# Attention and two expert layers on one core: the sixteenth tile's places are scattered alone, and the list scheduler gets new gaps and due times

## The chip, the cores and the metric

The kernel runs on one core of a Trainium2 chip. Its engines are TensorE (PE, matmuls; PEld is its weight load), VectorE (DVE), ScalarE (ACT), GpSimd (POOL) and SyncE (SP), which only issues transfers here. Each takes its instructions in the order in which they stand in the program. The metric is the device time of one execution in microseconds; the time before is the median of three runs.

## The reference, cut to what matters

Three layers follow one another; all arrays are float32.

```python
# attention: B, H, S, D = 4, 8, 576, 64; block-causal mask, blocks of 64
scores = scale * np.matmul(q, k.transpose(0, 1, 3, 2))
scores = np.where(mask, scores, -1000000000.0)
attn = np.exp(scores - scores.max(-1, keepdims=True))
attn = attn / (attn.sum(-1, keepdims=True) + 1e-09)
x = (attn @ v).transpose(0, 2, 1, 3).reshape(2304, 512)
# dense layer: w_in 512 x 1024, w_out 1024 x 512
h = x @ w_in
solu = h * softmax(h)
x = ((solu - mean(solu)) / np.sqrt(var(solu) + 1e-06) * g_ln) @ w_out
# experts: 8 of 512 x 1024 x 512, one for each token
logits = normed(x) @ normed(expert_emb).T / tau
expert_idx = np.argmax(logits, axis=1); gate_w = softmax(logits)[expert_idx]
out[mask] = gate_w[mask, None] * (np.maximum(x[mask] @ w1[e], 0.0) @ w2[e])   # for each expert e
```

## The kernel before, in words

Products are made with operands split in a high and a low half, three matmuls each (`mm3`, L552 to L557; "a triple" below is one such group on 512 columns, L555, L556, L557).

**The scheduled part.** Attention runs in 36 items (`items`): scores (`attn_score`, L436) with maximum (L439), exponential (L442) and scaling by the reciprocal sum (L448, L450, then `scaled`, L232 on ACT or L234 on POOL); transposes of the probabilities (`attn_trans`, L475, split at L481 and L484); the product with the values (`attn_av`, L520). The 2304 tokens are 18 tiles of 128. Each tile goes up (`b_load`, `b_up`, keys U: eight groups of triples, then maximum L600, exponential L601, product L603, normalization on POOL L606 and L610 to L614), down (`b_down`, D: transposes L631, eight triples, the tile stored to `x2d` at L641) and through the router (`b_route`, R: transposes L666, eight small products L675 and L676, a transposition L683, logits on DVE L686 and L687). The weights of the dense layer are unpacked meanwhile (`conv_ops`, C).

**Choosing.** Tiles are chosen for in batches (`BATCH`, L647). `b_choose` part 0 takes the roots of the norms on POOL (L705), the maximum, the one-hot matrix and the gate weights on DVE (L709 to L722); part 1 sums the one-hot matrices of the tiles before on POOL (`sums`, L730 to L733), turns them into places with two small products on TensorE (`places`, L737 and L738, "the place product" below), makes addresses on DVE (L747 to L749) and writes gate weight and token number of each tile to those places in the array `meta` in DRAM, one indirect transfer of POOL for a tile (L753, a "scatter"). All scatters write `meta`, so each waits until the one before has landed. The last batch that the scheduled part places holds tiles 12 to 15. Behind tile 15 (`TCUT`), `first_ops` counts tokens by expert (L797), picks the fullest (L804 to L810, L1092 to L1096), reads the first 2 x 128 places back from `meta` (SP, L979) and gathers these tokens' rows (POOL, L987).

**What sets the order.** All of this is written as operations with a duration, an engine, the names that they read and write, and for some a second engine that may take them (`either`). `order` walks through time and gives each engine the ready operation of highest priority; it reckons with `Rates`: `hop`, the gap from one engine's end to the next one's start, `over`, an engine's own gap, `land` and `rate` of transfers. A priority is the negative of a due time, `DUE` by kind of step and item, plus the step's own place in its chain (`priorities`). The sequence that comes out is the order of the instructions on each engine; the planner's times are not used on the chip, where every instruction waits for its real inputs. The planner also gives PSUM banks, and it decides who takes an `either`.

**The expert part** (`c_all`) works on slices of 128 gathered tokens: transposes L998, up (`c_up`, triples and L1016), transposes L1027, down (`c_down`), and a scatter of the rows to the output (L1044). The tiles 16 and 17 are chosen for inside its first slices. Its order is written out by hand. "The seam" below is the stretch from the last matmul of the scheduled part to the first L998.

Of the kernel before, what the change touches and what calls it, by code (L numbers as in the profile page):

```python
# [314 lines left out]
def conv_ops(c, k, n):  # L315
# [28 lines left out]
    op("POOL", 1.28, lambda: nc.gpsimd.tensor_tensor(WL, f, WH.bitcast(F32), op=ALU.subtract), r=[an, "wh%d" % k], w=["wl%d" % k],  # L344
# [21 lines left out]
def attn_prep(c, it):  # L366
# [30 lines left out]
    either(op, "POOL", lambda eng: scaled(c, eng, H, it.R, c.qscale[:, 0:1]), ACT=.21 + .00083 * W, POOL=.27 + .00083 * W,  # L397
# [9 lines left out]
def attn_prep_v(c, it):  # L407

    op, nc = c.op, c.nc
    k, n = 2 if it.low else 5, it.vi % 2  # L410
    raw = c.vraw[n][:, 0:k]
    op("SP", .45, lambda: nc.sync.dma_start(raw, c.v[it.pair, :, 0:k]), r=["pa"], w=["Vr%d" % n], size=64 * k)
    V = raw.rearrange("p c (h d) -> p c h d", d=64)
    V2 = c.V2[n][:, 0:k]
    vh, vl = V2[:, :, :, 0:64], V2[:, :, :, 64:128]
    either(op, "POOL", lambda eng: scaled(c, eng, vh, V, 1.0), ACT=.21 + .00083 * 128 * k, POOL=.2 + .00083 * 128 * k,
           r=["pa", "Vr%d" % n], w=["Vh%d" % n])
    op("POOL", .16 + .00219 * 128 * k, lambda: nc.gpsimd.tensor_tensor(vl, V, vh.bitcast(F32), op=ALU.subtract),
       r=["pa", "Vr%d" % n, "Vh%d" % n], w=["Vl%d" % n], lock=True)
# [5 lines left out]
def attn_score(c, it, step):  # L425
# [19 lines left out]
    if step in it.norm:  # L445
# [5 lines left out]
        for j in js:  # L451
            W, P, e = it.q[j][2:5]
            f = lambda eng, j=j, P=P, o=E[:P, e:e + W]: scaled(c, eng, o, o, rs[:P, j:j + 1])
            either(op, "POOL", f, ACT=.21 + .00083 * W, POOL=.28 + .00083 * W, r=["pa", ("rs%d" % n, a, b)], w=[(en, e, e + W)])
# [41 lines left out]
def attn_av(c, it, step):  # L496
# [34 lines left out]
    if odd:  # L531
        if two:
            op("POOL", .1 + .00208 * m, lambda: nc.gpsimd.tensor_tensor(xo[0], xo[0], xo[1], op=ALU.add), r=["pa", reg[1](0, 2)],
               w=[reg[0](0, 2)], lock=True)
# [38 lines left out]
def b_load(c, t):  # L573
# [8 lines left out]
    either(op, "POOL", lambda eng: scaled(c, eng, xh, xf, 1.0), ACT=.64, POOL=.63, r=[("xf%d" % n, 0, 4)], w=["xh%d" % n])  # L582
# [4 lines left out]
def b_up(c, t):  # L587
# [30 lines left out]
    op("POOL", 1.2, variance, r=[mn + "3", mn + "5", "mhalf"], w=[mn + "8"])  # L618
# [28 lines left out]
BATCH = [0, 4, 8, 12, 16, 17, 18]  # L647
# [43 lines left out]
def b_choose(c, a, part):  # L691
# [12 lines left out]
    if part == 0:  # L704
        op("POOL", .6, lambda: G.tensor_tensor(nr[:, 0:n], nr[:, 0:n], c.halves[:, 0:n], op=ALU.pow), r=["half"],  # L705
# [5 lines left out]
        op("DVE", .42, inverse, r=["tau", ("nr%d" % x, 0, 4)], w=[nm("inv")])  # L711
# [498 lines left out]
def order(ops, rate=Rates, tail=None):  # L1210
# [49 lines left out]
    now = 0.  # L1260
    while True:
# [39 lines left out]
        o.end = t + o.dur  # L1301
        free[o.eng] = o.end + rate.over[o.eng]
# [23 lines left out]
def stages(c, dag):  # L1326
# [30 lines left out]
    for t in range(NTILE):  # L1357
# [27 lines left out]
    Z=[163.2],  # L1385
    X=[766.1],
    C=[-186.4, 225.8, -38.9, -183.2, -79.3, -57.4, -32.7, -168.4, 102.7, 37.7, 153.1, 43.3, 136.9, 366.2, 97.9, -90.8],
    A=[-40.9, -100.2, -174.4, -308., -398.2, -149.3, -202.6, 49.4, -64.5, 40.3, -41.2, 363.3, 21.7, -200.9, 37.2, 224.4, -59.4,
       274.5, 333.9, -112.2, 441.1, 305.8, 242.1, -84.4, -110.4, -102.1, 198.1, 465.9, 430.9, 458.7, 662.3, 517.2, 529., 196.4,
       514.2, 899.3],  # L1390
    S=[-105.3, -140.4, -213.8, -231.1, -388., -122.3, 102.1, 10.4, 12.7, 71.1, 251.4, 207.4, 151.4, 53.2, 121.8, 98.8, 62.,
       175.8, 211., 189.6, 142.6, -5.8, 157.5, 90.4, 141.7, 104.5, 192.9, 185., 184.7, 115.2, 275.5, 391.6, 335.6, 245.6, 431.,
       323.1],
    T=[30.1, -109.5, -53., -143.6, -202.3, -105.5, -8.9, 108.5, -79.2, 179.9, 82.8, 93.7, -18.5, 4.6, 109.8, 147., -34., -76.8,
       -72.4, -29.4, 101.6, 126.4, 163.1, 90.1, 92.4, 161.1, 197.4, 233.6, 200.8, 256.6, 187.6, 280.3, 56.8, 49.9, 214.4,
       449.2],
    V=[-34.1, -143.2, 70.5, -217.7, -287., 46.9, 110.9, 24.8, 106.3, 53.2, -70.7, 168.4, 113.6, 22.7, 57.3, 147.5, 83.2, -106.6,
       -17.7, 28.5, 135.5, 142.7, 103.2, 218.3, 263.9, 191.7, 213.3, 155.6, 343., 349.7, 446.3, 630.1, 446.1, 332.9, 538.2,
       328.6],
    U=[-9.8, 72.8, -76.1, 195.2, -188.3, 52.3, 251.4, 242.9, 243.8, 325.4, 349.3, 352., 420.6, 454.4, 337.6, 239.3, 446.5,  # L1400
       856.5],
    D=[128.7, 209.1, 150.2, 236.2, 248., 260.7, -167.9, 257.5, 295.3, 373.9, 443., 589.1, 568.9, 326.3, 481.1, 143., 45.7,
       789.9],
    R=[-21.6, 42.5, 70.4, 237.8, 90.2, -283.1, -132.9, 25.4, 127.2, 774.6, 352.1, 140.5, 216.2, 934.2, 450.8, -49.4, 37.1,
       433.8],)
# [156 lines left out]
```

## Time and profile before

| what | value |
|---|---|
| median of 3 runs | 828.52 us (827.42 to 830.83) |
| profiled execution | 826.53 us, its span 824.6 us |
| TensorE busy in the span | 717.0 us (87%) |
| DVE, ACT, POOL busy | 471.0, 432.2, 330.4 us (57%, 52%, 40%) |
| mean granted TensorE clock | 0.946 |

The profile is of one execution. Busy times are sums over its span; the time of a single stretch is read from the windows and timelines below, since the stretches have different limits. "Idle before" in a row is the time in which the engine stood before this instruction, and behind the arrow is what ended it. The granted clock is the share of TensorE's full 2.4 GHz; 0.50 is its lower level, 1.2 GHz.

### The profile page before, as it was taken

To read this page: it belongs to the slowest core of one execution; us is meant where nothing else is said; L and a number is where in the kernel's file an instruction comes from. 1 tells how busy PE (TensorE), PEld (TensorE's weight loads), DVE (VectorE), ACT (ScalarE), POOL (GpSimd) and SP (SyncE) were. 2 spreads that over 40 slices of the span, in tenths; PEclk is the share of its full clock that TensorE was granted. 3 is DMA by queue.
4 is the path that set the end of the run, shared out by engine and by line. 5 is a ranking of instruction groups with operands and counts; after the bars stand their busy time and mean duration, and the time that the engine had idled before them with its cause. 6 is when DMAs were issued, how large, how long until landed. Compare 5 with 4: busy or idle time off the path is not lost. (4 is left out here: it accounts for less than half of the span.)

```text
span 824.6 us, 12837 instructions
## 1 busy us (share of the span) xinstructions
PE 717.0 (87%) x3830; PEld 576.5 (70%) x3830; DVE 471.0 (57%) x1040; ACT 432.2 (52%) x997; POOL 330.4 (40%) x512
## 2 busy tenths in 40 slices
PE   3869768889999899989999998099899989989994
PEld 2657556678777688768888786077688867867883
DVE  6778768777668587856884576053121256266221
ACT  6776668586786577756783564022121256165211
POOL 5564546666474465655454542212111101111110
PEclk9979779999999899999999999589999998999998
DMA  7974675534352435551112530108611137348110
GB/s 246 274 200 142 188 201 138 152 97 119 99 151 61 82 92 155 144 115 37 42 49 66 155 114 23 28 4 286 226 53 39 41 135 271 114 160 301 40 41 23
DMA packets 59891, 101.02 MB, mean 122 GB/s; under 512 B 14289, under 2 KB 26225, under 8 KB 59793
## 3 DMA queue, kind: packets, MB, share of 16 engines
q1 hardware_dynamic: 55856, 89.44, 37.2%
q0 software_dynamic: 3936, 10.51, 3.8%
q8 instruction: 32, 0.52, 0.3%
q14 instruction: 67, 0.54, 0.2%
HBM read 65.42 MB, written 15.11 MB: 98 GB/s over the span
## 5 line engine op out<-in xcount | busy, mean ns | idle before, releaser
L555 PE MATMUL banks<-wexp,workr 128*128 128x512 f32 x320 | 134.7, 421 | 3.7 <-ACTq L1056 3.0
L556 PE MATMUL banks<-wexp,workr 128*128 128x512 f32 x320 | 128.8, 402 | 3.7 <-DVEq L1056 3.7
L557 PE MATMUL banks<-wexp,workr 128*128 128x512 f32 x320 | 128.7, 402 | 0.0
L555 PE MATMUL banks<-win,workr 128*128 128x512 f32 x288 | 124.4, 432 | 0.7 <-ACT att L442 0.7
L543 DVE TENSOR_TENSOR workr<-banks,workr 128x512 fp32r<-128x512 f32 x61 | 42.2, 691 | 135.7 <-ACT workr L542 111.2
L436 PE MATMUL banks<-attr 128*64 128x512 f32 (+5 forms) x384 | 89.9, 361 | 30.2 <-DVE attr L392 11.5
L556 PE MATMUL banks<-win,workr 128*128 128x512 f32 x288 | 115.6, 402 | 0.0
L557 PE MATMUL banks<-win,workr 128*128 128x512 f32 x288 | 115.4, 401 | 0.0
L442 ACT ACTIVATE att<-banks,att 64x576 f32<-64x576 f32 (+4 forms) x160 | 90.1, 567 | 34.7 <-DVE att L439 33.1
L439 DVE TENSOR_REDUCE att<-banks 64x1 f32<-64x576 f32 (+4 forms) x160 | 82.7, 537 | 40.0 <-PE banks L436 37.4
L436 PEld LDWEIGHTS banks<-attr 128*128 128x128 f32 (+1 forms) x384 | 60.0, 196 | 46.0 <-POOL attr L388 11.5
L1016 ACT ACTIVATE work<-banks 128x512 f32<-128x512 f32 x40 | 23.9, 597 | 118.3 <-PE banks L557 118.2
L520 PE MATMUL banks<-attr 128*128 128x320 f32 (+9 forms) x504 | 71.9, 292 | 14.1 <-DVE attr L484 10.6
L1044 POOL DMA_INDIRECT out<-work x20 | 20.3, 1017 | 157.9 <-DVE work L1043 145.9
L475 PE MATMUL banks<-work,att 128*128 128x128 f32 (+1 forms) x480 | 72.5, 282 | 12.2 <-ACT att L232 4.5
L481 ACT ACTIVATE attr<-banks 128x320 fp32r<-128x320 f32 (+4 forms) x160 | 62.8, 434 | 35.1 <-PE banks L475 32.7
L520 PEld LDWEIGHTS banks<-attr 128*128 128x128 f32 (+1 forms) x504 | 65.9, 163 | 21.2 <-DVE attr L484 6.3
L484 DVE TENSOR_TENSOR attr<-banks,attr 128x320 fp32r<-128x320 f32 (+4 forms) x160 | 72.7, 481 | 11.5 <-ACT attr L481 9.8
L542 ACT ACTIVATE workr<-banks 128x512 fp32r<-128x512 f32 x61 | 36.5, 598 | 73.8 <-PE banks L1027 48.6
L475 PEld LDWEIGHTS banks<-work,att 128*128 128x128 f32 (+1 forms) x480 | 52.4, 150 | 31.6 <-issue 8.1
L556 PEld LDWEIGHTS banks<-wexp,workr 128*128 128x128 f32 x320 | 62.0, 194 | 17.0 <-DVEq L1056 5.2
L555 PEld LDWEIGHTS banks<-wexp,workr 128*128 128x128 f32 x320 | 61.7, 193 | 16.8 <-ACTq L1056 4.1
(210 smaller groups left out, 1289.6 us busy)
## 6 DMA issues: line engine op xcount, KB each, us to landing
raw<-in_w SPq DMA_DIRECT2D x28, 1024.0 KB, 8.1
attr<-attr SPq DMA_DIRECT2D x128, 144.0 KB, 3.4
att<-in_kq SPq DMA_DIRECT2D x32, 288.0 KB, 3.7
att<-in_v SPq DMA_DIRECT2D x16, 320.0 KB, 3.6
x2d<-work SPq DMA_DIRECT2D x19, 256.0 KB, 3.0
work<-xT SPq DMA_DIRECT2D x14, 256.0 KB, 3.2
work<-in_w_in SPq DMA_DIRECT2D x5, 512.0 KB, 5.7
xT<-att SPq DMA_DIRECT2D x16, 160.0 KB, 2.6
```

What stands on the lines that cost most here:

```text
L436: nc.tensor.matmul(ps.ap[:P, a:b], st[:, q0:q0 + P], mv[:, k0 + a:k0 + b], start=y == 0, stop=y == 1, skip_group_check=True)
L439: op("DVE", .15 + .00104 * W, lambda j=j, W=W, P=P, ps=ps: nc.vector.reduce_max(nm[:P, j:j + 1], ps.ap[:P, 0:W], axis=X, negate=True), r=[ ...
L442: op("ACT", .45 + .00086 * W, lambda j=j, W=W, P=P, e=e, ps=ps: nc.scalar.activation(E[:P, e:e + W], ps.ap[:P, 0:W], AF.Exp, bias=nm[:P, j ...
L475: nc.tensor.transpose(ps.ap[:, o:o + Q], E[:Q, a:a + 128], c.ident[:Q, :Q])
L481: op("ACT", .18 + .00083 * nch * Q, lambda src=src, dh=dh: nc.scalar.activation(dh(), src(), AF.Copy), r=["pa", ps], w=[("TH", a, b) for a ...
L484: lambda src=src, dh=dh, dl=dl: nc.vector.tensor_tensor(dl(), src(), dh().bitcast(F32), op=ALU.subtract),
L520: nc.tensor.matmul(o, a, b, start=k == 0, stop=k == len(mm) - 1, skip_group_check=True)
L542: h = c.nc.scalar.activation(H, ps, AF.Copy)
L543: return h, c.nc.vector.tensor_tensor(L, ps, H.bitcast(F32), op=ALU.subtract)
L555: nc.tensor.matmul(o, ah, bh, start=first, stop=False)
L556: nc.tensor.matmul(o, ah, bl, start=False, stop=False)
L557: nc.tensor.matmul(o, al, bh, start=False, stop=last)
```

## The change

One entry is added to `BATCH`, so that tile 15 has a batch of its own: its roots, sums, place product, addresses and scatter are separate operations now, and those of tiles 12 to 14 no longer wait for tile 15. The rest changes numbers of the planner: durations of some operations (the square root of a batch by its size, ACT's scaling 0.085 us more, POOL's steps), smaller hops between engines, an extra gap ahead of POOL, a negative own gap of ACT and DVE, landing 2.5 and rate 280 instead of 1.9 and 230, 0.07 us when TensorE changes from one kind of step to another, no hop behind operations without an engine, and a new value for every due time.

```diff
-BATCH = [0, 4, 8, 12, 16, 17, 18]
+BATCH = [0, 4, 8, 12, 15, 16, 17, 18]
...
-    either(op, "POOL", lambda eng: scaled(c, eng, H, it.R, c.qscale[:, 0:1]), ACT=.21 + .00083 * W, POOL=.27 + .00083 * W,
+    either(op, "POOL", lambda eng: scaled(c, eng, H, it.R, c.qscale[:, 0:1]), ACT=.295 + .00083 * W, POOL=.27 + .00083 * W,
...
-        op("POOL", .6, lambda: G.tensor_tensor(nr[:, 0:n], nr[:, 0:n], c.halves[:, 0:n], op=ALU.pow), r=["half"],
+        op("POOL", .4 + .16 * n, lambda: G.tensor_tensor(nr[:, 0:n], nr[:, 0:n], c.halves[:, 0:n], op=ALU.pow), r=["half"],
...
-    hop = dict(PE=.25, ACT=.1, DVE=.1, POOL=.12, SP=.1)
-    land, rate = 1.9, 230.
-    over = dict(PE=0., ACT=.02, DVE=.02, POOL=.03, SP=0.)
+    hop = dict(PE=.25, ACT=.04, DVE=.05, POOL=.04, SP=.06)
+    over = dict(PE=0., ACT=-.1, DVE=-.08, POOL=.08, SP=0.)
+    pool, turn, land, rate = .12, .07, 2.5, 280.
...
-            s.avail = max(s.avail, o.end + (0. if same else rate.hop[o.eng] if o.eng in rate.hop else 0.))
+            s.avail = max(s.avail, o.end + (0. if same or o.eng is None else rate.hop[o.eng] + (rate.pool if s.eng == "POOL" else 0.)))
...
+        if e == "PE":
+            o.end += rate.turn if o.key[0] != kind else 0.
+            kind = o.key[0]
...
-    Z=[163.2],
-    X=[766.1],
+    Z=[586.3],
+    X=[2200.3],
...
```

**The order on POOL at the end of the scheduled part.** The first row below is the last of tile 17's small steps. L705 are the roots of tiles 16 and 17, L730 x1, L732 x3 and L733 the sums of the batch 12 to 15, the other L730 and L733 those of tiles 16 and 17; L753 x1 and x3 are the four scatters of tiles 12 to 15. Behind them come the branch on a wrongly guessed first expert, which begins with a load of ti, and the gathers (L987).

```order
L613 TENSOR_SCALAR work<-work 128x1
L705 TENSOR_TENSOR work<-work 128x1
L730 COPY work<-work 128x8
L732 TENSOR_TENSOR work<-work 128x8 x3
L733 TENSOR_TENSOR work<-work 128x8
L730 COPY work<-work 128x8
L753 DMA meta<-work 18432x2
L705 TENSOR_TENSOR work<-work 128x1
L733 TENSOR_TENSOR work<-work 128x8
L730 COPY work<-work 128x8
L753 DMA meta<-work 18432x2 x3
L770 TENSOR_LOAD ti
```

Now the same stretch begins with tile 17's normalization (L606); the first scatter of tiles 12 to 14 stands two rows ahead of these.

```order
L606 TENSOR_SCALAR work<-work 128x1024
L753 DMA meta<-work 18432x2
L610 TENSOR_SCALAR work<-work 128x1
L611 TENSOR_SCALAR work<-work 128x1
L612 TENSOR_TENSOR work<-work 128x1
L613 TENSOR_SCALAR work<-work 128x1
L705 TENSOR_TENSOR work<-work 128x1
L753 DMA meta<-work 18432x2
L730 COPY work<-work 128x8
L733 TENSOR_TENSOR work<-work 128x8
L730 COPY work<-work 128x8
L753 DMA meta<-work 18432x2
```

The second and third scatter of the batch 12 to 14 stand among L606, L610 to L613 and the root of tile 15 (L705); one scatter, that of tile 15, is left behind its sums (L730, L733; the second L730 is tile 16's). The root of tile 16 and the first gather follow it, the second gather stands behind the branch.

**The order on TensorE at the seam.** Before, the place product of the batch 12 to 15 (32 columns) and the count (L797) stand here, then three triples of tile 17, and the expert part begins (L998, behind the branch).

```order
L797 MATMUL banks<-work 128x8
L555 MATMUL banks<-win,workr 128x512
L556 MATMUL banks<-win,workr 128x512
L557 MATMUL banks<-win,workr 128x512
L555 MATMUL banks<-win,workr 128x512
L556 MATMUL banks<-win,workr 128x512
L557 MATMUL banks<-win,workr 128x512
L555 MATMUL banks<-win,workr 128x512
L556 MATMUL banks<-win,workr 128x512
L557 MATMUL banks<-win,workr 128x512
L818 UNCONDITIONAL_BRANCH
L998 MATMUL banks<-work 128x128 x4
```

Now the place product of tile 15 (8 columns) and the count stand earlier; these rows follow the count, and the transposes L666 are of tile 16's router.

```order
L797 MATMUL banks<-work 128x8
L555 MATMUL banks<-win,workr 128x512
L556 MATMUL banks<-win,workr 128x512
L557 MATMUL banks<-win,workr 128x512
L666 MATMUL banks<-work 128x128 x4
L555 MATMUL banks<-win,workr 128x512
L556 MATMUL banks<-win,workr 128x512
L557 MATMUL banks<-win,workr 128x512
L555 MATMUL banks<-win,workr 128x512
L556 MATMUL banks<-win,workr 128x512
L557 MATMUL banks<-win,workr 128x512
L555 MATMUL banks<-win,workr 128x512
```

Between the count and L998 there are eight triples now, one group of four transposes, eight router products and one L683, where there were three triples. Between the place product of tiles 12 to 14 and that of tile 15 stand fifteen triples, five groups of four transposes, eight router products and one L683. From the first L998 on TensorE's rows are the same in both.

In the whole order, L234 (scaling on POOL) stands 138 times before and 117 now, L232 (the same on ACT) 95 and 115 times; TensorE goes from one kind of step to another 406 times before and 390 now; behind the last L520 stand 88 triples of the dense layer before and 104 now.

## Rows read from the trace of the kernel before

**Rows 1.** Stage windows: start:end, length, busy us (count) by engine, PE clock, DMA share, GB/s

```profile
0.00:11.53 11.53, 0.00 (x0) 0.03 (x1) 6.95 (x17) 6.79 (x11) 6.34 (x24) 1.00 0.85 258
11.53:175.00 163.47, 127.04 (x683) 99.20 (x683) 124.16 (x269) 112.51 (x290) 94.20 (x134) 0.90 0.67 185
175.00:435.00 260.00, 249.20 (x1504) 205.21 (x1505) 187.19 (x425) 180.38 (x470) 146.97 (x247) 0.97 0.36 93
...
513.30:535.40 22.10, 0.00 (x0) 0.00 (x0) 1.60 (x13) 1.51 (x4) 7.09 (x9) 0.59 0.11 29
535.40:541.40 6.00, 5.28 (x18) 3.86 (x19) 1.18 (x4) 0.79 (x2) 0.30 (x1) 0.50 0.09 28
541.40:824.60 283.20, 257.50 (x1206) 206.15 (x1204) 103.92 (x197) 91.05 (x151) 42.85 (x43) 0.97 0.37 126
```

**Rows 2.** TensorE timeline at the seam: start, us, instruction, idle before and releaser

```profile
510.84 0.19 PE L737 MATMUL banks<-work 128*128 128x32 bf16 x1
...
512.89 0.40 PE L557 MATMUL banks<-win,workr 128*128 128x512 f32 x1
535.43 1.12 PE L998 MATMUL banks<-work 128*128 128x128 f32 x4 [22.14 <-DMA work<-x2d,work]
```

**Rows 3.** GpSimd timeline at the seam and behind it

```profile
513.53 1.08 POOL L753 DMA_INDIRECT meta<-work  x1 [3.05 <-DVE work L715]
...
518.09 1.07 POOL L753 DMA_INDIRECT meta<-work  x1 [2.19 <-DMA meta<-work]
522.12 0.98 POOL L753 DMA_INDIRECT meta<-work  x1 [2.97 <-DMA meta<-work]
526.31 0.97 POOL L753 DMA_INDIRECT meta<-work  x1 [3.21 <-DMA meta<-work]
531.86 1.06 POOL L987 DMA_INDIRECT work<-x2d,work  x1 [4.57 <-SPq L818]
...
541.10 1.02 POOL L753 DMA_INDIRECT meta<-work  x1 [6.88 <-DVE work L749]
```

**Rows 4.** DMA issues from 513 to 536 us: queue, count, median us to landing

```profile
meta<-work POOLq DMA_INDIRECT x4, 3.8
```

**Rows 5.** TensorE timeline: the place product of tile 16

```profile
539.96 0.23 PE L737 MATMUL banks<-work 128*128 128x8 bf16 x1
```

**Rows 6.** TensorE timeline: transposes, triples and router products

```profile
489.76 0.60 PE L631 MATMUL banks<-work 128*128 128x128 f32 x4
490.12 0.48 PE L555 MATMUL banks<-win,workr 128*128 128x512 f32 x1
...
490.89 0.39 PE L555 MATMUL banks<-win,workr 128*128 128x512 f32 x1
...
491.60 0.40 PE L555 MATMUL banks<-win,workr 128*128 128x512 f32 x1
...
495.81 0.22 PE L675 MATMUL banks<-workr 128*16 128x128 f32 x1
...
496.29 0.61 PE L666 MATMUL banks<-work 128*128 128x128 f32 x4
```

**Rows 7.** GpSimd timeline: the normalization of tile 17 and a root

```profile
500.06 1.13 POOL L606 TENSOR_SCALAR work<-work 128x1024 f32<-128x1024 f32 x1 [1.16 <-DVE work L616]
502.48 0.34 POOL L610 TENSOR_SCALAR work<-work 128x1 f32<-128x1 f32 x1 [1.29 <-ACT work L617]
...
503.84 0.26 POOL L613 TENSOR_SCALAR work<-work 128x1 f32<-128x1 f32 x1
...
514.90 0.57 POOL L705 TENSOR_TENSOR work<-work 128x1 f32<-128x1 f32 x1 [0.29 <-ACT work L725]
```

**Rows 8.** Waits of TensorE, 0 to 180 us: us in total, times, longest

```profile
PE banks L520 <- DVE attr L484: 10.6, 8, 2.1
PE banks L436 <- DMA attr<-attr: 5.2, 4, 2.5
```

**Rows 9.** Groups by line: ACT's scaling of scores

```profile
L232 ACT ACTIVATE att<-att 128x256 f32<-128x256 f32 (+4 forms) x72 | 40.9, 594 | 11.6 <-DVE att L450 11.0
```

More of the change, by code (lines that the diff above doesn't have):

```diff
@@ L343, in conv_ops @@
     op("ACT", .63, lambda: nc.scalar.activation(WH, f, AF.Copy), r=[an], w=["wh%d" % k])
-    op("POOL", 1.28, lambda: nc.gpsimd.tensor_tensor(WL, f, WH.bitcast(F32), op=ALU.subtract), r=[an, "wh%d" % k], w=["wl%d" % k],
+    op("POOL", 1.1, lambda: nc.gpsimd.tensor_tensor(WL, f, WH.bitcast(F32), op=ALU.subtract), r=[an, "wh%d" % k], w=["wl%d" % k],
        lock=True)
@@ L415, in attn_prep_v @@
     vh, vl = V2[:, :, :, 0:64], V2[:, :, :, 64:128]
-    either(op, "POOL", lambda eng: scaled(c, eng, vh, V, 1.0), ACT=.21 + .00083 * 128 * k, POOL=.2 + .00083 * 128 * k,
+    either(op, "POOL", lambda eng: scaled(c, eng, vh, V, 1.0), ACT=.295 + .00083 * 128 * k, POOL=.2 + .00083 * 128 * k,
            r=["pa", "Vr%d" % n], w=["Vh%d" % n])
@@ L453, in attn_score @@
             f = lambda eng, j=j, P=P, o=E[:P, e:e + W]: scaled(c, eng, o, o, rs[:P, j:j + 1])
-            either(op, "POOL", f, ACT=.21 + .00083 * W, POOL=.28 + .00083 * W, r=["pa", ("rs%d" % n, a, b)], w=[(en, e, e + W)])
+            either(op, "POOL", f, ACT=.295 + .00083 * W, POOL=.28 + .00083 * W, r=["pa", ("rs%d" % n, a, b)], w=[(en, e, e + W)])
 def attn_trans(c, it, step):
@@ L532, in attn_av @@
         if two:
-            op("POOL", .1 + .00208 * m, lambda: nc.gpsimd.tensor_tensor(xo[0], xo[0], xo[1], op=ALU.add), r=["pa", reg[1](0, 2)],
+            op("POOL", .21 + .00208 * m, lambda: nc.gpsimd.tensor_tensor(xo[0], xo[0], xo[1], op=ALU.add), r=["pa", reg[1](0, 2)],
                w=[reg[0](0, 2)], lock=True)
@@ L581, in b_load @@
         at += w
-    either(op, "POOL", lambda eng: scaled(c, eng, xh, xf, 1.0), ACT=.64, POOL=.63, r=[("xf%d" % n, 0, 4)], w=["xh%d" % n])
+    either(op, "POOL", lambda eng: scaled(c, eng, xh, xf, 1.0), ACT=.72, POOL=.63, r=[("xf%d" % n, 0, 4)], w=["xh%d" % n])
     op("POOL", 1.1, lambda: nc.gpsimd.tensor_tensor(xl, xf, xh.bitcast(F32), op=ALU.subtract), r=[("xf%d" % n, 0, 4), "xh%d" % n],
@@ L617, in b_up @@
     op("ACT", 1.25, lambda: nc.scalar.activation(c.sq, u, AF.Square, accum_out=sm[:, 3:4]), r=[un], w=[mn + "3"])
-    op("POOL", 1.2, variance, r=[mn + "3", mn + "5", "mhalf"], w=[mn + "8"])
+    op("POOL", 1.36, variance, r=[mn + "3", mn + "5", "mhalf"], w=[mn + "8"])
 def b_down(c, t):
@@ L710, in inverse @@
             V.reciprocal(inv, inv)
-        op("DVE", .42, inverse, r=["tau", ("nr%d" % x, 0, 4)], w=[nm("inv")])
+        op("DVE", .55, inverse, r=["tau", ("nr%d" % x, 0, 4)], w=[nm("inv")])
         def first():
@@ L1259, in order @@
             put(o)
-    now = 0.
+    now, kind = 0., None
     while True:
@@ L1400 @@
[L1400 to L1405, printed above, removed]
+    Z=[586.3],
+    X=[2200.3],
+    C=[89.4, 3221.8, 1160.3, 1215., 353.7, 158.8, 128., -212.6, 55.5, -24.8, 643.6, 74.1, 2554.7, 3606.7, 2173.5, 295.7],
```

31 lines of the change are left out of this document (18 added, 13 removed).

## The prediction

> **What bounds the kernel now.** I read the stage windows first, then TensorE's timeline at the seam between the two parts of the program, then GpSimd's timeline over the same stretch, and last the waits of TensorE in the attention stretch. In the windows [rows 1] the reader is to see which engine sets the time of each stretch. TensorE (PE) is busy 249.20 of 260 us between 175 and 435 us and 257.50 of the last 283.20: there the kernel is bound by matmuls that neither table of numbers can remove. It is not busy in three places: the first 11.53 us; 163.47 - 127.04 = 36.4 us of the stretch up to 175 us; and the seam, 22.10 us with no matmul at all, behind which the clock is granted at 0.50 (1.2 instead of 2.4 GHz) for 6 us.
>
> The seam is one wait: after the last matmul of the scheduled part at 512.89 TensorE stands for 22.14 us until the first gather has brought the tokens of the first expert slice [rows 2]. GpSimd's (POOL's) timeline says why [rows 3]: the places of tiles 12 to 15 are written by four scatters (L753) at 513.53, 518.09, 522.12 and 526.31, each issued only when the one before has landed; a scatter takes a median 3.8 us to land [rows 4]. From first to last they stand (526.31 - 513.53) / 3 = 4.26 us apart. Only behind the fourth may the metadata be read and the gather (531.86) go.
>
> **The change, part by part.**
>
> *The seam.* Batch 12 to 15 is split into 12 to 14 and 15. The scatters of 12 to 14 no longer need tile 15's logits, and the new order puts three of them between the steps of tile 17's normalization on POOL, so that one scatter is left behind tile 15's places. Worked out from TensorE's place product of tile 15 (first L737 of the second batch in the new order):
> - From place product to scatter: tile 16's own batch shows it, product at 539.96 [rows 5], scatter at 541.10 [rows 3]: 1.14 us.
> - From the last scatter to the first transposes of the expert part: 535.43 - 526.31 = 9.12 us [rows 2, 3], unchanged in kind.
> - So the expert part starts 10.26 us behind that product. The new order has eight triples of matmuls behind it, one group of four transposes and eight router products (the single L683 I leave out). A triple takes 491.60 - 490.89 = 0.71 us, four transposes 490.12 - 489.76 = 0.36, the router products 496.29 - 495.81 = 0.48 [rows 6]: 8 x 0.71 + 0.36 + 0.48 = 6.5 us. They cover that much, and 3.7 us stay open.
> - Are the three scatters done in time? Between the two place products TensorE has 15 triples, five groups of transposes and one of router products: 10.65 + 1.80 + 0.48 = 12.9 us. On POOL the first scatter goes 1.14 us behind its product, or some 0.6 later because a maximum of tile 17 over 1024 columns stands ahead of its places on DVE (an estimate: half of the 1.13 us that L606 takes for as many columns [rows 7]). Three spacings of 4.26 put the fourth at 1.7 + 12.8 = 14.5, against 12.9 + 1.14 = 14.1 when its places are there. Between the scatters stand L606 (1.13 us), four small steps from L610 to L613 (503.84 + 0.26 - 502.48 = 1.62) and a root (0.57) [rows 7]; they fit into the landings, which POOL spends waiting today. I add 0.4 us: 4.1 us stay open instead of 22.14, a gain of **18.0 us**.
>
> The lower bound of this gain: if POOL comes so late that two of the three scatters still queue behind tile 15's product, 2 x 4.26 = 8.5 us are lost and 9.5 are left. The upper bound is no open gap, 22 us. I take 18.0, since each term has a row of its own kind. On the landing, the row shows 3.8 us [rows 4]. The Trainium skill, "DMA: Bandwidth & Descriptors", section "Anatomy of one DMA — SWDGE (gpsimd) path", gives a fixed cost of about 2.0 us for such a transfer, most of it the receipt of the write. The trace does not agree on the size for this scatter; by the page's figure a spacing would be about 3 us (an estimate), the three spacings taken out would be worth some 9 instead of 12.8, and the gain of the seam nearer 14.
>
> *The clock behind the seam.* For 6 us at 0.50 with 5.28 us busy [rows 1], at most 2.6 us can come back. Waits of 1 to 2.5 us stand in the attention stretch, whose clock is 0.90, so a short gap is no guarantee: I take 1.0, bounds 0 and 2.6.
>
> *Step changes.* The planner now charges TensorE 0.07 us for a change of kind, and the order changes kind less often: counted on the rows of the order by line groups, 406 times before and 390 after. The triple right behind transposes took 490.89 - 490.12 = 0.77 against 0.71 [rows 6]: 0.06 x 16 = **1.0 us** gained, bounds 0 and 2.
>
> *The new due times and gaps in the attention part.* Nothing is added or removed there, only moved: work of engines, transfers on SP, and the choice of engine. On the rows, 21 scalings go from POOL (138 to 117 of L234) to ACT (95 to 115 of L232). TensorE's idle in that stretch is made of short waits, as 10.6 us in 8 for L484 and 5.2 in 4 for small copies [rows 8], that is, of products put a microsecond too early for what they wait for. Gaps that are nearer to the chip's can turn some of that into work. Against this stands that ACT is busy 112.51 of 163.47 and 180.38 of 260 us (69% in both) and gets 21 x 0.594 us [rows 9] = 12.5 us more. The trace of before cannot show the result of so many moves. From below: half of the 36.4 us of idle goes, 18 us gained. From above: a loss of 12.5 us, if ACT's extra work is all on the path. I take a gain of **3 us**, near the middle of these, and keep both ends. The list's other numbers (durations, landing 2.5 instead of 1.9) make nothing run that has not run before.
>
> *The expert part.* TensorE's rows from the first L998 on are the same in both. 0.
>
> The sum: 18.0 + 1.0 + 1.0 + 3 = 23.0 us. The profiled execution took 826.53 us (span 824.6); less 23.0 is 803.5. The median of the timed runs lies 2.0 above the profiled execution, at 828.52; less 23.0 is 805.5. I predict **805.5 us**.
>
> **Rivals.**
> 1. *POOL comes late.* All between the scatters must run in POOL's order; a scatter that waits for a landing holds back tile 17's variance, and the variance holds back the next scatter. For it: POOL waits some 3 us at every scatter today [rows 3]. Against it: 12.9 us of matmuls stand beside the chain. Two spacings late: 805.5 + 8.5 = 814.
> 2. *The attention stretch gains much.* Half of its idle goes: 18 instead of 3 us, 790.5. For it: the waits there are short and many. Against it: DVE is busy 124.16 of 163.47 us there, 76%, with no work taken from it.
> 3. *Attention is paced by ACT, and the kernel becomes slower.* The new order ends attention with more of the dense layer's matmuls still to come: behind the last L520 stand 104 triples, 88 before, so 16 x 0.71 = 11.4 us of filler is taken out of attention. If ACT's chain and not TensorE sets the pace there, ACT's 12.5 us more at its share of 69% cost 18 us, and the 11.4 us come on top at the end: 29.5 us lost against a gain of 20.0 from the seam, clock and step changes, that is 838. It decides from 20 us on. Against it: from 175 to 435 us TensorE is at 96% and ACT at 69%, so ACT has room. A mild form, only the 12.5 us, gives 808.5 + 12.5 = 821.
> 4. *The split does nothing*, since the first gather waits for something else, as the branch that released POOL at 531.86 [rows 3]. That branch follows SP's reading of the metadata, which waits for the last scatter; 18 us would be lost, 823.5.
>
> **How the numbers follow.** Forecast 0.58 (798 to 811); rival 1 0.12; rival 2 0.11; the mild form of rival 3 0.09, its full form 0.05; rival 4 0.05. A measurement of this kernel can tell about 0.5%, 4.1 us, from no change. Faster by over that means below 824.4: forecast, rivals 1 and 2, most of the mild 3 and half of 4, 0.91. Within it 0.04, slower 0.05. The range for 8 in 10 takes in the forecast, rival 1 and part of 2 and of mild 3: 793 to 819.
>
> **What would show it.** In the profile after: one L753 instead of four between the last matmul of the scheduled part and the first gather; a wait of L998 for the gather of 2 to 7 us instead of 22.14; the clock behind it above 0.50. The three earlier scatters some 4.3 us apart with L606 and L610 between them. TensorE's idle up to 175 us between 18 and 49 us. The forecast is wrong if the wait stays above 12 us, if the last TensorE instruction ahead of the seam does not come near 513.3 - 4 = 509 us, or if the gain at the seam is eaten by waits of TensorE for ACT in attention.

## The result and the profile after

The changed kernel takes 806.67 us in the median of four runs (806.25 to 808.63), the kernel before beside it 829.67 (827.42 to 833.5): a ratio of 0.972 with an interval of 0.968 to 0.977. 805.5 us were forecast. The profiled execution of after took 808.63 us, its span is 806.9, against 826.53 and 824.6 before: in this pair of profiles 17.9 us went (17.7 by the spans), not 23. The rest of the 23.0 between the medians is that the profiled execution of before was 3.1 us below its median and that of after 2.0 above its own. Ratios, here and below, leave out executions more than 1.5% above the fastest of the same kernel, which concerns three of the six of the kernel with two scatters left, its profiled one among them, whose median with them is 809.66 us.

The stage windows of after, cut at its own milestones (start:end, length, busy us and count by engine, granted clock, DMA share, GB/s), answer to [rows 1]:

```profile
0.00:12.39 12.39, 0.00 (x1) 0.00 (x1) 5.24 (x16) 5.97 (x9) 4.25 (x21) 1.00 0.77 199
12.39:175.00 162.61, 129.81 (x742) 104.61 (x743) 132.31 (x281) 126.02 (x325) 90.92 (x131) 0.93 0.67 184
175.00:423.00 248.00, 237.78 (x1439) 193.25 (x1438) 177.14 (x414) 176.69 (x457) 134.10 (x231) 0.98 0.37 102
423.00:506.31 83.31, 82.13 (x433) 64.26 (x431) 51.91 (x142) 38.54 (x76) 38.02 (x63) 1.00 0.27 83
506.31:510.72 4.41, 0.00 (x1) 0.00 (x1) 0.27 (x2) 0.69 (x1) 2.54 (x4) 0.91 0.39 125
510.72:516.70 5.98, 5.29 (x18) 3.85 (x19) 1.56 (x6) 1.41 (x4) 0.89 (x2) 0.50 0.10 39
516.70:806.90 290.20, 260.97 (x1206) 209.03 (x1204) 103.97 (x197) 90.95 (x151) 42.63 (x43) 0.95 0.36 123
```

The scheduled part ends at 506.31 instead of 513.29 us (7.0 gained), the seam is 4.41 instead of 22.14 us long (17.7 gained), and from the first L998 to the end it takes 806.9 - 510.72 = 296.2 us instead of 824.6 - 535.43 = 289.2 (7.0 lost). The 6 us behind the seam stand at 0.50 as before.

The three places of the seam follow, first TensorE's timeline of after (start, us, instruction, idle before and releaser), which answers to [rows 2] and [rows 5]:

```profile
484.23 0.19 PE L737 MATMUL banks<-work 128*128 128x24 bf16 x1
...
497.90 0.17 PE L737 MATMUL banks<-work 128*128 128x8 bf16 x1
...
502.51 0.23 PE L676 MATMUL banks<-workr 128*8 128x128 f32 x1 [0.99 <-DVE workr L550]
...
510.72 1.11 PE L998 MATMUL banks<-work 128*128 128x128 f32 x4 [4.41 <-DMA work<-x2d,work]
```

and GpSimd's, which answers to [rows 3]:

```profile
485.97 1.09 POOL L753 DMA_INDIRECT meta<-work  x1 [2.17 <-DVE work L749]
...
487.87 1.13 POOL L606 TENSOR_SCALAR work<-work 128x1024 f32<-128x1024 f32 x1 [0.54 <-DVE work L616]
490.06 1.01 POOL L753 DMA_INDIRECT meta<-work  x1 [1.07 <-DMA meta<-work]
...
495.36 1.07 POOL L753 DMA_INDIRECT meta<-work  x1 [2.09 <-DMA meta<-work]
...
499.79 1.02 POOL L753 DMA_INDIRECT meta<-work  x1 [2.08 <-DVE ef L810]
...
506.60 1.09 POOL L987 DMA_INDIRECT work<-x2d,work  x1 [5.18 <-DVE work L744]
```

Three scatters run beside matmuls, with L606 between two of them, and one is left behind tile 15's place product (L737 at 497.90). The last matmuls wait 0.99 us for a split at 502.51. The landing of a scatter is what it was [rows 4], here among the issues from 480 to 498 us:

```profile
meta<-work POOLq DMA_INDIRECT x3, 3.8
```

In the attention, waits of TensorE from 0 to 436 us (us in total, times, longest), which answer to [rows 8], and the group of ACT's scaling that answers to [rows 9]:

```profile
PE banks L475 <- POOL att L234: 5.5, 1, 5.5
...
PE banks L475 <- ACT att L232: 2.1, 3, 1.1
...
PE banks L520 <- DVE attr L484: 1.2, 3, 0.5
```

```profile
L232 ACT ACTIVATE att<-att 64x576 f32<-64x576 f32 (+4 forms) x82 | 48.1, 620 | 8.6 <-DVE att L450 8.3
```

The 10.6 us of L520 for L484 are down to 1.2; a single wait of 5.5 us for POOL has come instead, at 22.88 us, where attention starts. In all, from its first matmul to the seam TensorE's idle fell from 47.6 to 44.2 us and its busy time from 454.2 to 449.7 us, with a clock of 0.93 instead of 0.90 in the first stretch; the first matmul comes 0.9 us later.

Most of the loss is in the third slice of the expert part: from the first to the fourth L998 pass 555.20 - 510.72 = 44.5 us instead of 573.71 - 535.43 = 38.3, which is 6.2 of the 7.0. The instructions are the same and in the same order, but not the times of three queues. Before (timelines of GpSimd, SP and TensorE):

```profile
556.72 1.05 POOL L987 DMA_INDIRECT work<-x2d,work  x1 [7.52 <-PE banks L557]
...
557.88 2.66 SPq L831 DMA_DIRECT2D raw<-in_w  x4
...
560.18 0.66 PE L998 MATMUL banks<-work 128*128 128x128 f32 x4 [0.41 <-DMA work<-x2d,work]
```

After:

```profile
532.86 1.05 POOL L987 DMA_INDIRECT work<-x2d,work  x1 [8.29 <-DMA work<-meta]
...
533.20 2.78 SPq L831 DMA_DIRECT2D raw<-in_w  x4
...
539.61 1.11 PE L998 MATMUL banks<-work 128*128 128x128 f32 x4 [4.49 <-DMA work<-x2d,work]
```

L987 gathers the tokens of the third slice, L831 loads the next expert's weights (four transfers of 1 MB). Before, the gather had 1.16 us to itself; after, 0.34, and from its issue to the first transposes (L998) pass 6.75 instead of 3.46 us. TensorE stands for 4.49 instead of 0.41 us, and the transposes take 1.11 instead of 0.66 us, that is, at half clock.

### The profile page after: what moved, and what is told of

The parts are those of the page before. It is cut to its first block, busy times and chain, and to the rows that moved or that the text cites. A ratio compares the mean times of both kernels' runs of the same rounds, so it can differ in the third digit from the quotient of the medians.

```text
span 806.9 us, 12838 instructions
## 1 busy us (share of the span) xinstructions
PE 716.0 (89%) x3832; PEld 575.0 (71%) x3832; DVE 472.4 (59%) x1055; ACT 440.3 (55%) x1019; POOL 313.4 (39%) x493
## 5 line engine op out<-in xcount | busy, mean ns | idle before, releaser
L555 PE MATMUL banks<-wexp,workr 128*128 128x512 f32 x320 | 135.8, 424 | 3.6 <-ACTq L1056 2.9
L555 PE MATMUL banks<-win,workr 128*128 128x512 f32 x288 | 123.5, 429 | 2.6 <-POOL workr L234 1.6
L436 PE MATMUL banks<-attr 128*128 128x256 f32 (+5 forms) x384 | 88.8, 357 | 29.4 <-POOL attr L388 12.4
L436 PEld LDWEIGHTS banks<-attr 128*128 128x128 f32 (+1 forms) x384 | 57.5, 191 | 44.7 <-POOL attr L388 12.4
L439 DVE TENSOR_REDUCE att<-banks 64x1 f32<-64x576 f32 (+4 forms) x160 | 80.3, 534 | 12.9 <-PE banks L436 12.1
L475 PE MATMUL banks<-work,att 128*128 128x128 f32 (+1 forms) x480 | 69.2, 279 | 13.6 <-POOL att L234 5.5
L484 DVE TENSOR_TENSOR attr<-banks,attr 128x128 fp32r<-128x128 f32 (+4 forms) x160 | 70.7, 483 | 17.9 <-ACT attr L481 17.0
L520 PE MATMUL banks<-attr 128*128 128x320 f32 (+9 forms) x504 | 71.0, 288 | 6.5 <-DVE att L450 2.2
L520 PEld LDWEIGHTS banks<-attr 128*128 128x128 f32 (+1 forms) x504 | 65.5, 162 | 14.1 <-ACT att L442 4.1
L556 PEld LDWEIGHTS banks<-wexp,workr 128*128 128x128 f32 x320 | 62.5, 195 | 17.1 <-DVEq L1056 5.2
L555 PEld LDWEIGHTS banks<-wexp,workr 128*128 128x128 f32 x320 | 62.3, 195 | 16.9 <-ACTq L1056 4.0
L557 PEld LDWEIGHTS banks<-wexp,workr 128*128 128x128 f32 x320 | 61.9, 194 | 15.3 <-DVE workr L543 0.5
L475 PEld LDWEIGHTS banks<-work,att 128*128 128x128 f32 (+1 forms) x480 | 51.3, 148 | 28.2 <-POOL att L234 8.5
```

Source lines behind the costliest of these rows:

```text
L436: nc.tensor.matmul(ps.ap[:P, a:b], st[:, q0:q0 + P], mv[:, k0 + a:k0 + b], start=y == 0, stop=y == 1, skip_group_check=True)
L439: op("DVE", .15 + .00104 * W, lambda j=j, W=W, P=P, ps=ps: nc.vector.reduce_max(nm[:P, j:j + 1], ps.ap[:P, 0:W], axis=X, negate=True), r=[ ...
L475: nc.tensor.transpose(ps.ap[:, o:o + Q], E[:Q, a:a + 128], c.ident[:Q, :Q])
L484: lambda src=src, dh=dh, dl=dl: nc.vector.tensor_tensor(dl(), src(), dh().bitcast(F32), op=ALU.subtract),
L520: nc.tensor.matmul(o, a, b, start=k == 0, stop=k == len(mm) - 1, skip_group_check=True)
L555: nc.tensor.matmul(o, ah, bh, start=first, stop=False)
```

## The experiments

Three groups of kernels, each timed beside the kernel before on one chip (its medians there: 825.77, 826.46 and 825.09 us). The first group holds the split alone, the numbers alone, late weights and the changed kernel; the second two scatters left, the old due times, the added matmuls and both edits together, without the changed kernel; the third the new due times, both together and the changed kernel. Theory: the seam is the chain of scatters, the split shortens it, the planner's numbers move the attention; the third slice is a race of two transfers. The rivals stand with each. One table first; "scheduled end" is the first L998 less its wait, all times but the ratio are from the profiled execution:

| kernel | ratio to before (95%) | scheduled end | wait at the seam | wait of third L998 | first L998 to the end |
|---|---|---|---|---|---|
| before | 1 | 513.3 | 22.14 | 0.41 | 289.2 |
| changed | 0.972 (0.968 to 0.977) | 506.3 | 4.41 | 4.49 | 296.2 |
| changed, group 1 | 0.966 (0.962 to 0.969) | 500.0 | 4.38 | 0.61 | 290.5 |
| changed, group 3 | 0.970 (0.965 to 0.975) | 502.7 | 2.97 | 2.67 | 292.7 |
| split only | 0.999 (0.998 to 1.001) | 520.1 | 11.06 | 0 | 289.8 |
| numbers only | 0.982 (0.979 to 0.985) | 503.8 | 18.24 | 0 | 287.5 |
| old due times | 1.011 (1.008 to 1.014) | 518.6 | 23.77 | 1.79 | 291.4 |
| new due times, old gaps | 1.023 (1.019 to 1.027) | 543.8 | 4.71 | 0 | 288.3 |
| two scatters left | 0.971 (0.966 to 0.976) | 508.7 | 6.61 | 4.60 | 294.7 |
| late weights | 0.962 (0.959 to 0.965) | 501.9 | 2.44 | 0.54 | 286.5 |
| added matmuls | 0.960 (0.957 to 0.963) | - | 0.38 | 0 | 286.8 |
| both, group 2 | 0.958 (0.954 to 0.962) | - | 0.42 | 0 | 282.9 |
| both, group 3 | 0.965 (0.961 to 0.968) | - | 0 | 0.37 | 285.1 |

### The split alone

```diff
 # in the kernel before
-BATCH = [0, 4, 8, 12, 16, 17, 18]
+BATCH = [0, 4, 8, 12, 15, 16, 17, 18]
```

> The kernel before with the batch split alone. The planner with its old numbers puts the two place products side by side, so all four scatters still stand behind them, with eight triples beside them instead of three. If the seam is the chain of scatters: 1.2 + 3 x 4.26 + 9.1 = 23.1 us behind the product, some 6 us of matmuls beside it, a wait of 17 us instead of 22.1, a total of 5 us less, about 824. If the split by itself frees the chain (the reading in which the due times matter little): a wait of 4 to 8 us and 812 to 816.

826.12 us (822.36 to 827.14, 12 runs), no change, where 824 was expected. In the profile the wait at the seam is 11.1 us shorter (11.06 us, 17 expected), but the scheduled part 6.8 us longer; this execution, at 823.0 us, was 3.1 below the median. TensorE's rows:

```profile
503.40 0.17 PE L737 MATMUL banks<-work 128*128 128x24 bf16 x1
...
505.84 0.17 PE L737 MATMUL banks<-work 128*128 128x8 bf16 x1 [1.62 <-DVE work L718]
...
512.14 0.79 PE L557 MATMUL banks<-win,workr 128*128 128x512 f32 x1 [2.70 <-DVE workr L550]
...
531.16 1.12 PE L998 MATMUL banks<-work 128*128 128x128 f32 x4 [11.06 <-DMA work<-x2d,work]
```

The old due times put both place products side by side (503.40 and 505.84), so all four scatters (510.54, 514.70, 518.65, 522.39) still stand behind the last one; TensorE merely meets the wait earlier, in pieces such as these 1.62 and 2.70 us and at half clock. The split by itself is worth nothing.

### The numbers alone

```diff
 # in the changed kernel
-BATCH = [0, 4, 8, 12, 15, 16, 17, 18]
+BATCH = [0, 4, 8, 12, 16, 17, 18]
```

> The changed kernel with the old batches, 12 to 15 together. If the seam is the chain of scatters: four scatters behind the place product, seven triples and the router of tile 16 beside them, a wait of 18 to 19 us; the scheduled part ends near 506 us as in the changed kernel (7 us earlier than before); total 829.7 - 3.5 - 7 = 818 to 821. If the new numbers do the work by themselves: below 812.

811.2 us (810.62 to 811.85), 14.6 us faster than before by the medians. That is below the 812 set for the rival, that the new numbers do the work by themselves; but the wait of the first L998 stays, as the theory had it, and what was mis-sized is the gain elsewhere:

```profile
497.43 0.19 PE L737 MATMUL banks<-work 128*128 128x32 bf16 x1
...
522.00 1.12 PE L998 MATMUL banks<-work 128*128 128x128 f32 x4 [18.24 <-DMA work<-x2d,work]
```

The place product of tiles 12 to 15 comes 6.3 us ahead of the scheduled end (497.43 to 503.8) and the wait is 18.24 us. With the split on top (the changed kernel beside it, 797.41 us) another 13.8 us go, close to the difference of the two waits, 18.24 - 4.38 = 13.9. In the two profiles the rest nearly cancels: the scheduled part ends 3.8 us earlier (503.8 and 500.0), the part from the first L998 on is 3.0 us longer (287.5 and 290.5).

### Two scatters left instead of one

```diff
 # in the changed kernel
-BATCH = [0, 4, 8, 12, 15, 16, 17, 18]
+BATCH = [0, 4, 8, 12, 14, 16, 17, 18]
```

> The changed kernel, but the batch is cut one tile earlier (12 and 13 | 14 and 15 instead of 12 to 14 | 15), so that two scatters and not one are left behind the last place product. The matmuls stay in the same order. Theory (the seam is the chain of scatters behind the last place product, 4.3 us each): the wait of the first L998 becomes 4.4 + 4.3 = 8.7 us and the kernel 4.3 us slower than the changed one, a ratio to the kernel before some 0.005 higher than the changed kernel's. Rival (the wait for the gather is set by something else than the count of scatters left, since three terms of my sum were each 2 us off): the wait stays at 4.4 us and the time within 1 us.

The ratio of 0.971 lies among the changed kernel's three (0.966, 0.970, 0.972), so in time nothing can be told. In the profile the wait is 6.61 us, between the two expectations; GpSimd's timeline:

```profile
502.10 1.08 POOL L753 DMA_INDIRECT meta<-work  x1 [1.78 <-DVE amf L806]
...
505.98 1.04 POOL L753 DMA_INDIRECT meta<-work  x1 [2.17 <-DVE rowbuf L921]
511.94 1.05 POOL L987 DMA_INDIRECT work<-x2d,work  x1 [4.92 <-SPq L818]
```

The second scatter costs its spacing, 3.88 us, but the way from the last scatter to the first L998 is shorter here, 515.28 - 505.98 = 9.30 instead of 10.93 us. That way was 9.12 us before [rows 2, 3], 10.89 and 9.49 in the two other executions of the changed kernel: a term that varies by 1.8 us hides part of what I wanted to see. The direction speaks for the chain of scatters, the size is not shown.

### Old due times with the new gaps, and new ones with the old gaps

```diff
 # the changed kernel, all of it but
 DUE = dict(
-    Z=[586.3],
-    X=[2200.3],
+    Z=[163.2],
+    X=[766.1],
...
```

> The changed kernel with the due times of the kernel before: new durations, gaps, landings and step changes, and the batch split. Both place products stand next to each other again, so the wait at the seam should be 11 to 18 us, as where the split alone was made. What it tells is the scheduled part. Theory A (the gain up to the seam comes from the due times): the last L520 of the attention comes at about 432 to 435 us, as in the kernel before. Theory B (it comes from the measured gaps and durations, which choose the engine and put waits where they are): the last L520 comes at 408 to 418 us, as in the changed kernel. In the whole: A about 826, B about 812 us where the kernel before takes 826.

```diff
 # the kernel before, with the split and
 DUE = dict(
-    Z=[163.2],
-    X=[766.1],
+    Z=[586.3],
+    X=[2200.3],
...
```

> The kernel before with the new due times and the batch split, but with the old durations, gaps and landings and without the step change. Theory (due times and planner's numbers belong together: the due times carry the gain, but fit only the times that the planner reckons with, as old due times with new numbers were 9 us slower than the kernel before): the last L520 comes later than the changed kernel's 408 to 414 us, by 3 to 10 us, and the kernel takes 805 to 820 us where the kernel before takes 826. Rival (the due times do all of it): last L520 at 408 to 414 us and the changed kernel's time within 2 us.

Old due times: 835.79 us (833.45 to 838.84), 9 slower than before; the last L520 starts at 436.6 us (435.8 before, 415.6 in the changed kernel), near the 432 to 435 of theory A, but the total was expected at 826. New due times with old gaps: 843.34 us (838.5 to 848.61), 18 slower than before, outside the 805 to 820 expected; the last L520 starts at 435.9, so the due times do not carry the gain alone either. The theory behind that run, that the two belong together, holds, and its size was off by 23 us. Where TensorE waits up to 436 us (us, times, longest), with the old due times:

```profile
PE banks L475 <- ACT att L232: 10.7, 5, 6.2
PE banks L436 <- DMA attr<-attr: 9.3, 4, 4.8
PE banks L475 <- DVE attr L484: 7.3, 4, 4.2
```

and with the new ones and the old gaps:

```profile
PE banks L475 <- ACT att L232: 11.3, 7, 3.4
PE banks L475 <- POOL att L234: 10.1, 10, 2.3
...
PE banks L436 <- DMA attr<-attr: 7.5, 5, 3.5
```

The transposes (L475) come too early for the scaling in both, by 10.7 and 11.3 us for ACT alone; in the kernel before it was 4.5, in the changed one 2.1 us. These waits are a part of it. From its first matmul to the end of the scheduled part TensorE is idle for 56.3 us with the old due times and for 70.2 with the new ones and the old gaps, against 47.6 before, and busy for 449.4 and 465.8 against 454.2. The last L520 was a poor gauge: with the new due times and the old gaps 118 triples are left behind it, before 88 and in the changed kernel 104.

The seam goes the other way. It stays at 23.77 us with the old due times, where 11 to 18 were expected, and closes to 4.71 us with the new ones, even under the old gaps: with the split, the order that the new due times make is enough to close it, and the scheduled part loses more than that gains (30.5 us longer). In time neither half is a gain: the due times are an answer to one set of gaps, and with another set they are worse than the pair before. Which of the gaps matters most was not tried.

### The changed kernel again, twice

No edit. First and third group:

> The changed kernel unaltered, a second profile. Theory A (a race between the third gather and the loads of the second expert's weights costs the expert part some 4 us of wait and 3 us of half clock in the first profile, and comes out differently from execution to execution): the wait of the third L998 is anywhere between 0.4 and 4.5 us, the time 804 to 809 us. Theory B (that wait belongs to the new order): 4 to 5 us again. In both the wait at the seam is 4 to 5 us and the last matmul of the scheduled part stands near 506 us.

> The changed kernel as it is, beside the others of this call on one chip. Ratio to the kernel before 0.964 to 0.974. Theory on its spread (same order, but in some executions TensorE's clock falls to 0.50 behind a short wait near 104 us and near 350 us and costs 3 and 2 us, and the third gather loses 4 us to the weight loads): executions differ by up to 10 us, while those of the kernel before differ by up to 7.

797.41 us (794.5 to 802.26) and 799.73 us (795.6 to 806.95). The first lies below the 804 to 809 us that both theories had; the ratio of the second is in the range expected, and its executions differ by 11.4 us, those of the kernel before beside it by 8.9. In the profile of the first group the race of the third slice is not lost:

```profile
526.24 1.10 POOL L987 DMA_INDIRECT work<-x2d,work  x1 [7.67 <-PE banks L557]
...
527.18 2.54 SPq L831 DMA_DIRECT2D raw<-in_w  x4
...
529.72 0.66 PE L998 MATMUL banks<-work 128*128 128x128 f32 x4 [0.61 <-DMA work<-x2d,work]
```

The weights start 0.94 us behind the gather and the way to L998 is 3.48 us. Over the ten profiles in which the weights are loaded there, the three above among them, the way from the gather's issue to L998 was 6.75, 6.95 and 5.23 us where the weights started 0.34, 0.54 and 0.64 us behind it, and 3.3 to 3.6 us where they started 0.94 to 2.1 us behind, with one exception (1.32 and 4.94, with the old due times).

The scheduled part ends 6.3 us earlier than in the first profile of the same kernel. The timelines of TensorE show one of the places. First profile, then group 1:

```profile
105.97 0.76 PE L436 MATMUL banks<-attr 128*64 128x512 f32 x4 [1.14 <-DVE workr L550]
...
107.49 0.63 PE L555 MATMUL banks<-win,workr 128*128 128x512 f32 x1
...
118.07 0.50 PE L555 MATMUL banks<-win,workr 128*128 128x512 f32 x1
```

```profile
107.02 0.77 PE L436 MATMUL banks<-attr 128*64 128x512 f32 x4 [1.13 <-DVE workr L550]
...
108.41 0.40 PE L555 MATMUL banks<-win,workr 128*128 128x512 f32 x1
...
115.84 0.50 PE L555 MATMUL banks<-win,workr 128*128 128x512 f32 x1
```

The order and the waits ahead are the same (1.14 and 1.13 us for L550), but in one execution a matmul of 512 columns takes 0.63 and in the other 0.40 us: from L436 to the same L555, 118.07 - 105.97 = 12.1 against 115.84 - 107.02 = 8.8 us. Around 350 us, behind waits of 1.84 and 1.43 us for L484, another 2.2 us are lost in the same way. That is the spread of this kernel; both losses were in the first profile.

### Late weights

```diff
 # in the changed kernel, expert part
-            if s == 0:
-                e = c_reg(c, c.tab[0:1, 97:98], [ENG.SP], 0, NE - 1)
+            if s == 1:
...
+                nc.vector.scalar_tensor_tensor(t2, c.s[2]["xl"][0:1, 0, 0:1].bitcast(F32), 0.0, c.rows["tot"][:, 1:2], op0=ALU.mult, op1=ALU.add)
+                nc.vector.tensor_copy(t3, t2)
+                e = c_reg(c, t3[0:1, 0:1], [ENG.SP], 0, NE - 1)
                 c_wload(c, e, 1, 1)
...
```

To the number of the expert 0 times a value of the third slice's split is added, so that SP waits for that split.

> The changed kernel, with the loads of the second expert's weights held until the third slice's rows are split (two 1x1 operations on DVE make the register's source depend on it). Theory A (the third gather shares the transfer engines with 4 MB of weights that start 0.3 us after it): the third L998 waits 0 to 1 us instead of 4.49, no half clock behind it, the expert part 5 to 7 us shorter than the 296.2 us of the first profile, total 800 to 803. Theory B (the gather is late by itself, or the weights are needed sooner): no gain, 806 to 808, or later waits for the weights.

794.9 us (791.14 to 797.8), 2.5 us under the changed kernel beside it, with overlapping intervals; 800 to 803 were expected. From the first L998 to the end 286.5 us against 290.5, but the third L998 waited little in both (0.54 and 0.61): the 4 us are behind it, where the waits for the weight swaps (L1056) sum to 4.3 instead of 6.6 us. Two of these waits, in the changed kernel of group 1:

```profile
551.46 0.50 PE L556 MATMUL banks<-wexp,workr 128*128 128x512 f32 x1 [1.35 <-DVEq L1056]
...
559.00 0.50 PE L555 MATMUL banks<-wexp,workr 128*128 128x512 f32 x1 [1.02 <-ACTq L1056]
```

With the weights held back TensorE waits for nothing in this stretch. From the fourth to the sixth L998 pass 28.0 us in each of the ten profiles without this edit, and 25.1 us in each of the three with it (both together are the other two): 2.9 us that the edit gains whether the race is lost or not. What the race costs stands in the first profile; that holding the weights back ends it is likely, since from the third gather's issue to L998 pass 3.42, 3.44 and 3.62 us in these three profiles, but no two runs that differ in this alone show it: in group 1 it was not lost without the edit either.

### Matmuls in the gap, and both together

```diff
 # in the changed kernel, c_all
...
     c_miss(c)
+    fill = c.ps.tile([128, 512], F32, tag="acc", name="fill", bufs=2)
+    for _ in range(16):
+        nc.tensor.matmul(fill, c.W1H[0][:, 0:128], c.W1H[0][:, 0:512], start=True, stop=True)
     c_in(c, 0)
```

The added products are never read.

> The changed kernel with 16 matmuls of 128x128 by 512 columns added that compute nothing that is used, between the last matmul of the scheduled part and the first L998, where TensorE stands 4.4 us. Theory (the clock falls to 0.50 because TensorE stands still, and costs up to 2.6 us in the 6 us behind): granted clock above 0.9 in the 6 us behind the first L998, the expert part 1.5 to 2.6 us shorter. Rival (the 6 us at half clock are paced by the gathers and evictions of the first slices, and not by matmuls): the clock is up and the expert part is as long as before, within 0.5 us.

794.26 us (791.72 to 797.75). The stretch from the first L998 on, in windows of this kernel and of the changed one in group 1:

```profile
506.94:513.00 6.06, 5.37 (x32) 3.77 (x33) 1.87 (x5) 2.01 (x4) 1.07 (x1) 1.00 0.07 26
```

```profile
504.34:510.30 5.96, 5.27 (x18) 3.83 (x19) 1.56 (x6) 1.54 (x4) 1.01 (x2) 0.52 0.11 34
```

The clock is 1.00 instead of 0.52, and 32 instead of 18 matmuls run in 6 us. From the first to the third L998 pass 529.37 - 506.94 = 22.4 us instead of 529.72 - 504.34 = 25.4; 0.6 of these 3.0 us are the wait of the third. So the half clock behind the seam costs 2.4 us, close to the 2.6 that I took as its upper bound, and TensorE kept busy gives it back. It stands between the first and the second L998: 9.28 us here and 9.29 and 9.22 in the two profiles of both edits together, against 11.29, 11.66 and 10.70 in the three of the changed kernel. In the time of the whole kernel this is not shown by itself, as no changed kernel ran beside this one: its ratio is 0.960, those of the changed kernel 0.966 to 0.972.

> Both: the added matmuls in the open gap, and the loads of the second expert's weights held behind the split of the third slice. If both gains are there, 2 us from the clock and 1 to 6 us from the gather that no longer runs beside 4 MB of weights, the kernel takes a ratio of 0.958 to 0.966 to the kernel before on this chip, and the third L998 waits under 1 us. If the weights matter only in some executions, it lies within 1 us of the kernel with the added matmuls alone.

> The changed kernel with the added matmuls in the gap at the seam and the second expert's weight loads held back, beside the changed kernel on one chip. Expected 5 to 9 us faster than the changed kernel in this call: 3.7 us from the clock behind the seam, 3.9 from the third slice. Rival (the gains were those of one profile): within 2 us of it.

795.29 and 794.99 us. In group 3, 4.7 us under the changed kernel beside it by the medians (5 to 9 were expected), though the two intervals overlap. In the profiles the expert part is 282.9 and 285.1 us, against 290.5, 292.7 and 296.2 in the three of the changed kernel. In time it cannot be told from either edit alone: its ratios are 0.958 and 0.965, those of the added matmuls and of late weights 0.960 and 0.962, and in group 2 its median is 1.0 us above that of the added matmuls. Between its two profiles the first L998 stands 6.3 us apart and the part behind it 2.2, so most of that difference comes from the scheduled part, which neither edit touches.

## Why the prediction came out

**The seam, 18.0 us: right in sum (17.7), in two of its terms wrong.** From tile 15's place product to the first L998 I had 1.14 + 9.12 = 10.26 us; it was 510.72 - 497.90 = 12.8, since the scatter at 499.79 came late (1.89 instead of 1.14) and the way behind it took 10.93. Its row names DVE's L810, but its addresses (L749) were done at 498.73 and it stands 4.43 us behind the scatter before it, a spacing of the chain, so it was the landing that held it. That is what came of rival 1, POOL late: 0.75 us, not 8.5. On the other side the eight triples were not 6.5 but 506.31 - 497.90 = 8.4 us long, with 0.99 us of waiting among them. The two errors cancel: 4.41 against 4.1. The scatters stood 4.09, 5.30 and 4.43 us apart where I had 4.26, and the place products 13.7 where I had 12.9, again one error against the other. The landing of 3.8 us that I took from the row held. From the 2.0 us of fixed cost in the Trainium skill's "DMA: Bandwidth & Descriptors", section "Anatomy of one DMA — SWDGE (gpsimd) path", I had estimated spacings of 3 us and a gain nearer 14; the trace does not agree on the size, with 3.8 us to the landing, spacings of 4.09 to 5.30 us and a gain of 17.7.

**What I credited to the split is the split in the new order.** Without the new numbers it gives nothing in time; with them it gives 13.8 us, and the numbers alone 14.6. I had 18 and 4 (with the step changes). Of the 14.6 us, 22.14 - 18.24 = 3.9 are a shorter wait at the seam, 513.3 - 503.8 = 9.5 the scheduled part and 289.2 - 287.5 = 1.7 the part behind, by the profiles. Rival 4 (the split does nothing) was wrong for the changed kernel, and right for the split by itself, for another reason than mine.

**The half clock, 1.0 us: wrong, 0.** I took 1.0 between 0 and 2.6, from waits of 1 to 2.5 us that stand in attention at a clock of 0.90. Nothing came back: behind the waits of 4.41, 4.38 and 2.97 us in the three profiles the next 6 us were granted 0.50, 0.52 and 0.71, and behind 2.44 us (late weights) 0.52. Only without a gap was it 1.00.

**Attention and step changes, 3 + 1 us: right sign, mis-sized.** 7.0, 13.3 and 10.6 us in the three profiles. The mechanism that I named, waits that turn into work, gave 47.6 - 44.2 = 3.4 us in the first of them, and 1.0 and 4.4 in the others (idle 46.6 and 43.2). The larger part is busy time, 454.2 us before and 449.7, 441.6 and 447.1 after, for 2608 and 2610 matmuls. I put it down to the clock, since the three executions after are of one program and differ by 8.1 us in it: 0.93, 0.95 and 0.94 in the first stretch instead of 0.90, and 0.98 to 1.00 instead of 0.97 in the second. That part was not in my sum; 0.06 us for each of 16 step changes is 1.0 of it at most. Why the new order keeps the clock up more often is shown by no run here and stays open. ACT did take more work (126.02 of 162.61 us, 78%, in the first stretch) and TensorE waited for its scaling 2.1 us up to 436 us, instead of 4.5: rival 3 falls. Rival 2's size (18 us) was nearer than mine for the second of these profiles (13.3), not for the other two.

**The expert part, 0: wrong, 7.0 us lost in the first profile, 1.3 and 3.5 in the others.** That TensorE's rows are the same in both was true and said nothing on two other queues that start transfers within a microsecond of each other. I had compared TensorE's rows alone, not when SP's and POOL's transfers start.

So the median was met within 1.2 us by errors that cancel: 1.0 too much for the clock and up to 7.0 for the expert part on one side, 3.0 to 9.3 too little for attention on the other. That closeness is luck: the changed kernel lay 28.4 and 25.4 us under the kernel before in the two later timings. The sign rested on the one term of 18 us, and that was right.

## What to carry to other kernels

A planner's gaps and its due times are one thing: here each without the other was slower than the kernel before, the gaps by 9 us and the due times by 18, so they are changed and measured together, and a structural edit is judged only in the order that was made for it. When a wait is moved or removed, look at the three queues behind it for transfers that now start side by side, not only at the engine that sets the time. A gap at a seam costs twice, once for its length and once for the clock behind it (2.4 us here), and matmuls that nobody reads bought the second part back. The last instruction of one kind says little on an order if the work left behind it differs: compare idle and busy time up to a point that both orders share.

## What the runs showed that I had not expected

The same program, with the same order and the same waits (1.14 and 1.13 us), ran on at clock 1.00 in one execution and at 0.50 from 107 to 117 us in another, which cost 3.3 us; what decides is open. A small gather issued 0.3 to 0.6 us ahead of 4 MB of weights took 5.2 to 7.0 us to reach TensorE, and 3.3 to 3.6 us when it had 0.9 us or more for itself, but for one case. Both make single profiles of this kernel differ by up to 12 us, more than several of the terms that I argued over.
